# The last half pair's softmax sums are inverted on chip instead of through DRAM

## The chip, the cores and the metric

The kernel runs on one core of a Trainium2 chip. The metric is the device time of one execution in microseconds. A core has five engines with queues of their own: PE (TensorE, matmul), DVE (VectorE), ACT (ScalarE), POOL (GpSimd) and SP (SyncE, which here only issues DMAs). Each works through its queue in order, and semaphores tell one engine when another, or a DMA, is done.

## The reference

Attention with a bucket mask over 4 batches, 8 heads, 768 positions and 64 features, and behind it a gated MLP (gMLP) per batch of 768 x 512:

```python
mask = q_bucket[:, :, :, None] == k_bucket[:, :, None, :]
scores = scale * np.matmul(q, k.transpose(0, 1, 3, 2))
scores = np.where(mask, scores, -1000000000.0)
scores = scores - np.max(scores, axis=-1, keepdims=True)
attn = np.exp(scores)
attn = attn / (np.sum(attn, axis=-1, keepdims=True) + 1e-09)
x = np.matmul(attn, v)                # then heads are put side by side: (4, 768, 512)

h = x @ w_in                          # 512 -> 1024
h = 0.5 * h * (1.0 + np.tanh(c * (h + 0.044715 * h ** 3)))
u, v = (h[..., :d_ff // 2], h[..., d_ff // 2:])
v_n = (v - mu) / np.sqrt(var + 1e-06) * g_ln
v_s = np.einsum('ts,bsd->btd', w_sg, v_n) + b_sg[None, :, None]
out = x + (u * v_s) @ w_out
```

The division by the row sums is what the change touches, for 1/32 of the rows.

## The kernel before

**Attention.** Heads are worked in 16 pairs (two heads fill 128 partitions), each pair in two halves of 384 queries. For each half, `weigh` computes scores transposed (keys in partitions, queries in columns), takes the exponential on ACT into `p`, multiplies with v on PE (`av`), and adds the `p` tiles up on POOL and DVE into one `sum` tile for each head. `finish` then needs, for each query, the sum over all keys: a matmul of `sum` with a matrix of ones. Its steps (lines of the profile):

- `total` (L598): for each head the sums of 384 queries, as two times 192 columns, each copied to 32 partitions; ACT copies them to `sm` (L601), and `av` to `un` (L603).
- A trip through DRAM, to spread 768 values over all partitions: `s<-sm` (L606), `sq<-s` (L607, 128 partitions x 6 columns), 1e-9 is added (L608) and the reciprocal taken (L609) on DVE, `r<-sq` (L611), and two broadcasts `rs<-r` (L613, one for each head).
- `e` (L617, L618) on ACT, for queries that match no key; `xt = un * rs` (L619) on DVE; `xt + e` (L620) on POOL; and `xs<-xt` (L621), which stores the half's result, transposed, in DRAM.

All DMAs of this trip are issued on SP, between the loads of q, k, v and of `x`.

**MLP.** For each of the 4 batches, `load_x` loads four x tiles (L694, 128 features x 768 positions) and splits each into a high part `xh` (ACT, L699) and a low part `xl` (POOL, L697). `hidden` multiplies with w_in in three matmuls for each x tile: six tiles `ps_h` of 512 columns for the gate's input (L765), then eight of 384 columns for u (L794), with four PSUM buffers. A tile is freed once `gelu2` is done: the square `h` on ACT (L749), a product on DVE (L750), the tanh on ACT (L752), a product on DVE into `y` or `u` (L754). From y follow the normalisation (DVE L772 to L774, POOL L775, DVE L777) and its high and low parts `zh` (ACT L779) and `zl` (DVE L781). In batch 0, `gate_weights` loads w_sg into `gs` (L716, issued on ACT) and transposes it on PE (L724; ACT L730, DVE L733), b_sg goes through `gs` to `b_bc` (L707, L708), and `out_weights` splits w_out (loads `ow` L338; DVE L356 to L365; POOL L358). `gate` is L812 to L823, `project` L838 to L848, with loads `rx` (L834).

**What sets the order.** All steps are given to a planner (`Plan`), with engine, an assumed cost, a priority and the buffers read and written. It lays out each engine's queue once, from the assumed costs; on the chip the queues are fixed. Attention's SBUF pool `late` (sum, un, rs, e, xt and the p tiles) is closed when the last half pair is finished, and the MLP's pool `b3` (gs, wgh, woh, u, ow and others) opens in its place: what writes there waits for what was read there.

Of the kernel before, what the change touches and what calls it, by code (L numbers as in the profile page):

```python
# [9 lines left out]
F32 = mybir.dt.float32  # L10
# [5 lines left out]
ALU = mybir.AluOpType  # L16
# [16 lines left out]
class Plan:  # L33
# [38 lines left out]
    def add(self, engine, cost, prio, fn, r=(), w=(), dma=0, port=None, form=None, lat=0.0):  # L72

        port = engine == "POOL" if port is None else port
        g = {"e": engine, "c": cost, "p": prio, "fn": fn, "dma": dma, "n": len(self.groups), "slots": [], "port": port, "form": form, "lat": lat}
        deps, after = set(), set()
        for kind, xs in (("r", r), ("w", w)):
            for x in xs:
                b, key = x if isinstance(x, tuple) else (x, None)
                if b.slots is not None and engine != "MEM":  # L80
                    g["slots"].append(b)
                if b.first is None:
                    b.first = g["n"]
                    last, gone = b.prev
                    if b.need is not None:
                        deps.update(n for n, _, _ in b.need.uses)
                    if gone is not None:
                        gone.gone = True
                        deps.update(n for n, _, _ in gone.uses)
                    if last is not None and last.first != g["n"]:  # L90
                        after.add(last.first)
                elif b.first != g["n"]:
                    after.add(b.first)
                assert b.gone is False
                for n, k2, kind2 in b.uses:
                    if n != g["n"] and (kind == "w" or kind2 == "w") and (key is None or k2 is None or key == k2):
                        deps.add(n)
                b.uses.append((g["n"], key, kind))
        g["deps"], g["after"] = deps, after - deps
        self.groups.append(g)  # L100

# [121 lines left out]
def kernel(  # L223
# [16 lines left out]
    nc = tc.nc  # L240

    B, H, S, D = q.shape
    P = 128
    NT = S // P
    HT = NT // 2
    SH = S // 2
# [16 lines left out]
    QH2, W6 = SH // 2, SH // 64  # L263

    const = ctx.enter_context(tc.tile_pool(name="const", bufs=1))
    dram = ctx.enter_context(tc.tile_pool(name="dram", bufs=1, space=DRAM))
# [5 lines left out]
    nc.vector.tensor_copy(identr, ident)  # L272
    epsr = const.tile([P, 1], F32, name="epsr")
    nc.vector.memset(epsr, -0.5)
    ones = const.tile([P, 32], F32, name="ones")
    nc.vector.memset(ones, 1.0)
    less = const.tile([P, 1], F32, name="less")
    nc.vector.memset(less, -1.0)
# [89 lines left out]
    PE, DVE, ACT, POOL, SP = "PE", "DVE", "ACT", "POOL", "SP"  # L368
    xs = [[dram.tile([P, S], F32, name=f"xs_{b}_{hp}") for hp in range(NP)] for b in range(B)]

    plan = Plan()
# [45 lines left out]
    if True:  # L417
# [5 lines left out]
        def ps_tile():  # L423
            ps_s.list.append(plan.slot(ps_slots, lambda i: ps_s.pool.tile([P, 512], F32, tag=f"g{i}",
                                                                          name=f"g{i}_{len(ps_s.list)}", bufs=1)))
            return ps_s.list[-1]

        def dma(prio, us, fn, r=(), w=(), e=SP, lat=0.0):
            eng = nc.sync if e == SP else nc.scalar
            plan.add(e, 0.6 if e == ACT else 0.57, prio, lambda: fn(eng), r, w, dma=us, lat=lat)  # L430
# [14 lines left out]
        def row(j):  # L445
            return slice(j * D, (j + 1) * D)
# [100 lines left out]
        def weigh(st, hf, k0, prio):  # L547
# [28 lines left out]
            for i, kt in enumerate(two):  # L576
                if kt == 0:
                    continue
                e = ADDS[kt - 1]
                for j in range(2):  # L580
                    def add(j=j, i=i, e=e, first=p[0][j] if kt == 1 else sums[j]):
                        (nc.gpsimd if e == POOL else nc.vector).tensor_add(sums[j](), first()[:, :SH], p[i][j]()[:, :SH])  # L582

                    plan.add(e, 1.01 if e == POOL else 0.55, prio + 0.6, add, [p[i][j]] + ([p[0][j]] if kt == 1 else []),
                             [sums[j]], port=True)

        def finish(st, hf, prio):

            av, sums, tp = st.av, st.sum, ps_tile()
            sm, e = late.ring([P, QH2], F32, "sm", 3), late.ring([P, SH], F32, "e", 3)  # L590
            sq, rs, xt = late.ring([P, W6], F32, "sq", 3), late.ring([P, SH], F32, "rs", 3), late.ring([P, SH], F32, "xt", 2)
            V = nc.vector

            def total():
                for j in range(2):
                    for a in range(2):
                        r = 64 * j + 32 * a
                        nc.tensor.matmul(tp()[r:r + 32, :QH2], ones, sums[j]()[:, a * QH2:(a + 1) * QH2], start=True, stop=True)  # L598

            plan.add(PE, 0.6, prio, total, sums, [tp])  # L600
            plan.add(ACT, 0.32, prio, lambda: nc.scalar.copy(sm(), tp()[:, :QH2]), [tp], [sm])  # L601
            un = late.ring([P, SH + 1], F32, "un", 3)
            plan.add(ACT, 0.48, prio - 1, lambda: nc.scalar.copy(un(), av()[:, :SH + 1]), [av], [un])  # L603

            sd, sb = dram.tile([4, QH2], F32, name=f"s_{st.n}_{hf}"), plan.buf(f"s_{st.n}_{hf}", 1)
            dma(prio, 0.1, lambda eng: eng.dma_start(sd, sm()[0:P:32, :]), [sm], [sb], lat=3.6)  # L606
            dma(prio, 0.1, lambda eng: eng.dma_start(sq(), sd.rearrange("a (p c) -> (a p) c", c=W6)), [sb], [sq], lat=4.0)  # L607
            plan.add(DVE, 0.16, prio, lambda: V.tensor_single_scalar(sq(), sq(), 1e-9, op=ALU.add), [sq], [sq], port=True)  # L608
            plan.add(DVE, 0.18, prio, lambda: V.reciprocal(sq(), sq()), [sq], [sq])  # L609
            rd, rb = dram.tile([2, SH], F32, name=f"r_{st.n}_{hf}"), plan.buf(f"r_{st.n}_{hf}", 1)  # L610
            dma(prio, 0.1, lambda eng: eng.dma_start(rd.rearrange("j (p c) -> (j p) c", c=W6), sq()), [sq], [rb], lat=4.0)  # L611
            for j in range(2):
                dma(prio, 0.3, lambda eng, j=j: eng.dma_start(rs()[row(j)], rd[j].partition_broadcast(D)), [rb], [(rs, j)], lat=4.6)  # L613

            vm = late.ring([P, 1], F32, "vm", 3)
            plan.add(ACT, 0.2, prio, lambda: nc.scalar.mul(vm(), un()[:, SH:SH + 1], 1.0 / S), [un], [vm])
            plan.add(ACT, 0.62, prio, lambda: nc.scalar.activation(e(), rs(), AF.Relu, bias=less[:, 0:1], scale=2e-9), [rs], [e])  # L617
            plan.add(ACT, 0.62, prio, lambda: nc.scalar.mul(e(), e(), vm()[:, 0:1]), [e, vm], [e])  # L618
            plan.add(DVE, 0.56, prio, lambda: V.tensor_mul(xt(), un()[:, :SH], rs()), [un, rs], [xt], port=True)  # L619
            plan.add(POOL, 0.98, prio, lambda: nc.gpsimd.tensor_add(xt(), xt(), e()), [xt, e], [xt])  # L620
            dma(prio, 0.55, lambda eng: eng.dma_start(xs[st.b][st.hp][:, hf * SH:(hf + 1) * SH], xt()),  # L621
                [xt], [(xd[st.b][st.hp], hf)])

        NPAIR = B * NP
# [26 lines left out]
        for n in range(NPAIR):  # L651
            for c in range(NT):
                if c == 0:
                    prepare(n + 1)
                hf, k0, g = c // HT, 2 * (c % HT), NT * n + c
                maxima(g + AHEAD)
                weigh(sts[n], hf, k0, 2 * g)
                if c % HT == HT - 1:
                    finish(sts[n], hf, 2 * g + FINP)
# [192 lines left out]
    for b in range(B):  # L852
        p = 500 + 1000 * b
# [41 lines left out]
```

## Time and profile before

| | us |
|---|---|
| median of 3 runs | 833.68 |
| lowest and highest | 831.89, 835.25 |
| the profiled execution, its own time | 836.75 |
| its span, from the first to the last instruction | 834.9 |
| busy PE, DVE, ACT, POOL in it | 796.2, 602.9, 412.0, 391.7 |
| mean granted TensorE clock | 0.987 |

The profile is of one execution. Times in it count from the span's start. Attention's last matmul lies at 488 us, and the MLP follows to the end. A busy PE is not a PE at its peak, since matmuls overlap: the rate is read from the distance between starts. The granted clock is the share of full speed that the throttle allowed PE.

### The profile page before, as it was taken

How to read it: one execution, taken by the hardware profiler on the slowest of the kernel's cores; microseconds unless marked ns; L12 is line 12 of the kernel's file. 1: busy time of each engine (PE TensorE's matmuls, PEld its weight loads, DVE VectorE, ACT ScalarE, POOL GpSimd, SP SyncE). 2: the span in 40 equal slices, each digit the busy share in tenths (PEclk: the TensorE clock that was granted, in tenths of full speed). 3: DMA queues.
4: the chain of work that ended last, by engine and by line, in shares of the span. 5: the costliest groups of instructions: out<-in, count | busy, mean ns of one | idle time of the engine just before them, and what ended most of it. 6: DMA issues, size and time to landing. Idle time of an engine off the chain costs nothing.

```text
span 834.9 us, 15309 instructions
## 1 busy us (share of the span) xinstructions
PE 796.2 (95%) x5480; PEld 613.5 (73%) x5480; DVE 602.9 (72%) x1305; ACT 412.0 (49%) x926; POOL 391.7 (47%) x406
## 2 busy tenths in 40 slices
PE   7999999989999999999999988799899999999998
PEld 5776666656666667666666547789689989988996
DVE  7899899997999797677677539889944248516730
ACT  2565656645655656565656745533434135314511
POOL 0566766665765655675666862234204201611030
PEclk9999999999999999999999999799999999999999
DMA  6033233223324223213301233320033230131003
GB/s 164 14 80 81 70 81 103 74 77 77 85 60 121 61 60 87 67 52 85 87 28 41 88 108 115 128 67 29 26 108 101 70 101 1 38 102 51 1 1 126
DMA packets 99308, 60.94 MB, mean 73 GB/s; under 512 B 64288, under 2 KB 91040, under 8 KB 99232
## 3 DMA queue, kind: packets, MB, share of 16 engines
q1 hardware_dynamic: 97920, 56.94, 24.3%
q10 hardware_dynamic: 1312, 3.02, 1.1%
q8 instruction: 43, 0.70, 0.4%
q14 instruction: 33, 0.27, 0.1%
HBM read 47.16 MB, written 12.78 MB: 72 GB/s over the span
## 4 chain that ended last, share of the span: by engine, by line
PE 76%; DVE 16%; DMA 4%; issue 1%; SPq 1%; POOL 1%; ACT 1%; DVEq 0%; ACTq 0%; POOLq 0%
PE g L561 15%; PE av L573 14%; PE ps_vs L812 10%; PE g L517 8%; PE ps_o L838 8%; PE ps_h L794 6%; PE ps_h L765 4%; DVE mx L524 4%; PE g L497 4%; PE g L475 2%; PE g L539 1%; PE g L598 1%; PE ps_o L843 1%; DMA q<-in_q_dram 1%; DVE wx L359 1%
## 5 line engine op out<-in xcount | busy, mean ns | idle before, releaser
L582 POOL TENSOR_TENSOR sum<-sum,p 128x384 f32<-128x384 f32 x192 | 200.4, 1067 | 69.5 <-ACT p L567 40.9
L524 DVE TENSOR_REDUCE mx<-g 128x1 f32<-128x384 f32 x384 | 188.2, 548 | 52.8 <-PE g L517 52.6
L567 ACT ACTIVATE p<-g 128x384 f32<-128x384 f32 x384 | 159.4, 500 | 123.7 <-PE g L561 121.1
L573 PE MATMUL av<-p,v 128*64 128x385 f32 x768 | 146.7, 504 | 0.0
L582 POOL TENSOR_TENSOR sum<-p,p 128x384 f32<-128x384 f32 x64 | 64.4, 1027 | 62.9 <-ACT p L567 62.8
L573 PEld LDWEIGHTS av<-p,v 128*64 128x64 f32 x768 | 47.0, 136 | 54.4 <-issue 51.5
L750 DVE SCALAR_TENSOR_TENSOR h<-h,ps_h 128x384 f32<-128x384 f32 (+1 forms) x56 | 33.0, 607 | 74.0 <-ACT h L749 73.7
L517 PE MATMUL g<-fk,fq 64*128 64x384 f32 x384 | 76.3, 371 | 4.3 <-DVE mx L524 4.0
L561 PE MATMUL g<-hq,hk 64*128 64x384 f32 x384 | 77.7, 384 | 2.0 <-DVE mx L524 2.0
L561 PEld LDWEIGHTS g<-hq,hk 64*128 64x128 f32 x384 | 39.3, 188 | 41.4 <-DVE mx L524 20.9
L517 PE MATMUL g<-hk,hq 64*128 64x384 f32 x384 | 69.2, 337 | 0.0
L561 PE MATMUL g<-hq,lk 64*128 64x384 f32 x384 | 68.4, 338 | 0.0
L561 PE MATMUL g<-fq,fk 64*128 64x384 f32 x384 | 68.2, 337 | 0.0
L561 PE MATMUL g<-lq,hk 64*128 64x384 f32 x384 | 68.1, 337 | 0.0
L812 PE MATMUL ps_vs<-wgh,zh 128*128 128x384 f32 x192 | 64.6, 336 | 2.2 <-DVE gt L815 1.4
L775 POOL TENSOR_TENSOR mv<-mv,epsr 128x1 f32<-128x1 f32 x24 | 14.0, 584 | 111.4 <-DVE mv L774 103.1
L838 PE MATMUL ps_o<-woh,gs 128*128 128x512 f32 x192 | 65.5, 402 | 0.0
L812 PE MATMUL ps_vs<-wgh,zl 128*128 128x384 f32 x192 | 64.4, 335 | 0.7 <-DVE zl L781 0.7
L812 PE MATMUL ps_vs<-wgl,zh 128*128 128x384 f32 x192 | 64.2, 334 | 0.0
L517 PEld LDWEIGHTS g<-fk,fq 64*128 64x128 f32 x384 | 40.0, 184 | 32.5 <-ACT p L567 8.4
L823 POOL TENSOR_TENSOR gs<-gt,gs 128x384 fp32r<-128x384 f32 x32 | 32.8, 1028 | 61.7 <-ACT gs L820 61.7
L794 PE MATMUL ps_h<-xh,wih 128*128 128x384 f32 x128 | 45.2, 353 | 7.7 <-DVE y L754 4.0
(127 smaller groups left out, 1708.7 us busy)
## 6 DMA issues: line engine op xcount, KB each, us to landing
q<-in_q_dram SPq DMA_DIRECT2D x32, 192.0 KB
k<-in_k_dram SPq DMA_DIRECT2D x32, 192.0 KB
v<-in_v_dram SPq DMA_DIRECT2D x16, 384.0 KB
rs<-r SPq DMA_DIRECT2D x64, 96.0 KB
xs<-xt SPq DMA_DIRECT2D x32, 192.0 KB
x<-xs SPq DMA_DIRECT2D x16, 384.0 KB
rx<-xs SPq DMA_DIRECT2D x96, 64.0 KB
out_dram<-ob SPq DMA_DIRECT2D x24, 256.0 KB
```

The source lines that it names most:

```text
L497: nc.tensor.matmul(fp()[:, :SH], w[:, s, :], x()[:, cs], start=(i == 0), stop=(i == 2))
L517: nc.tensor.matmul(sc[kh][j]()[:, :SH], x[0]()[row(j), qs], x[1]()[row(j), kh * SH:(kh + 1) * SH], start=(n == 0), stop=(n == 1))
L524: plan.add(DVE, 0.56, prio, lambda j=j, kh=kh: nc.vector.tensor_reduce(mx()[:, kh, i, j:j + 1], sc[kh][j]()[:, :SH], axis=AX.X, op=ALU.max ...
L561: nc.tensor.matmul(sc[i][j]()[:, :SH], x()[row(j), ks], y()[row(j), cs], start=(n == 0), stop=(n == 3))
L567: plan.add(ACT, 0.53, prio, lambda i=i, j=j: nc.scalar.activation(p[i][j]()[:, :SH], sc[i][j]()[:, :SH], AF.Exp), [sc[i][j]], [p[i][j]])
L573: nc.tensor.matmul(av()[row(j), :SH + 1], st.v()[:, j, kt, :], p[i][j](), start=(kt == 0), stop=(kt == NT - 1))
L582: (nc.gpsimd if e == POOL else nc.vector).tensor_add(sums[j](), first()[:, :SH], p[i][j]()[:, :SH])
L750: plan.add(DVE, us + 0.07, prio, lambda: nc.vector.scalar_tensor_tensor(h2()[:, :n], h2()[:, :n], 1.0 / GA, ps()[:, :n], op0=ALU.add, op1= ...
L765: nc.tensor.matmul(ps(), x()[:, ts_], w[:, c, FH:FF], start=(c == 0 and n == 0), stop=(c == NC - 1 and n == 2))
L794: nc.tensor.matmul(ps()[:, :SH], w[:, c, fs], x()[:, cs], start=(c == 0 and n == 0), stop=(c == NC - 1 and n == 2))
L812: nc.tensor.matmul(vp(), z()[:, t, fs], w()[:, t, cs], start=(t == 0 and n == 0), stop=(t == NT - 1 and n == 2))
L838: nc.tensor.matmul(po(), a()[:, ts_], w()[:, f, :], start=(f == 0 and n == 0), stop=False)
```

## The change

For the second half of the last pair (`quick`), `total` gives the sums of all 384 queries of a head in one matmul to all 64 partitions of that head (so `ones` has 64 columns instead of 32). DVE adds 1e-9 out of PSUM into `rs` and takes the reciprocal there, in all 384 columns. The copy to `sm`, the two DVE instructions on `sq` and the five DMAs of the trip fall away for this half. The other 31 halves are done as before, the first half of the same pair too. A line in the planner keeps a step from depending on itself.

```diff
-    ones = const.tile([P, 32], F32, name="ones")
+    ones = const.tile([P, D], F32, name="ones")
...
+            quick = st.n == NPAIR - 1 and hf == 1
+            if quick:
+                def whole():
+                    for j in range(2):
+                        nc.tensor.matmul(tp()[row(j), :SH], ones, sums[j](), start=True, stop=True)
+
+                plan.add(PE, 0.75, prio, whole, sums, [tp], form="col")
+                plan.add(DVE, 0.55, prio, lambda: V.tensor_single_scalar(rs(), tp()[:, :SH], 1e-9, op=ALU.add), [tp], [rs])
+                plan.add(DVE, 2.5, prio, lambda: V.reciprocal(rs(), rs()), [rs], [rs], port=True)
+            else:
                 def total():
...
             un = late.ring([P, SH + 1], F32, "un", 3)
             plan.add(ACT, 0.48, prio - 1, lambda: nc.scalar.copy(un(), av()[:, :SH + 1]), [av], [un])
+            if not quick:
                 sd, sb = dram.tile([4, QH2], F32, name=f"s_{st.n}_{hf}"), plan.buf(f"s_{st.n}_{hf}", 1)
                 dma(prio, 0.1, lambda eng: eng.dma_start(sd, sm()[0:P:32, :]), [sm], [sb], lat=3.6)
...
                 for j in range(2):
                     dma(prio, 0.3, lambda eng, j=j: eng.dma_start(rs()[row(j)], rd[j].partition_broadcast(D)), [rb], [(rs, j)], lat=4.6)
```

The planner lays out the queues anew. Up to the last half pair's `total` they are the same on every engine; from there on they differ at some places. Lines of the changed file stand 1 to 13 further down (L762 is the old L749, L765 in its ACT rows the old L752, L778 the old L765, L807 the old L794). The numbers behind the names tell buffers apart: h_0, h_1, h_2 are the first MLP tiles in the GELU, e_7276 and e_7229 belong to the first half of the last pair, e_7240 to the second.

ACT, behind the split of batch 0's last x tile, before:

```order
L699 CAST xh_7216<-x_7189 128x768
L749 ACTIVATE h_0_7245<-ps_h_7205 128x512
L749 ACTIVATE h_1_7255<-ps_h_7218 128x512
L752 ACTIVATE h_0_7245<-h_0_7245 128x512
L752 ACTIVATE h_1_7255<-h_1_7255 128x512
L617 ACTIVATE e_7276<-rs_7231,less 128x384
L618 ACTIVATE e_7276<-e_7276,vm_7135 128x384
L749 ACTIVATE h_2_7294<-ps_h_7251 128x512
```

Here the GELU of two tiles stands ahead of the first half's e. ACT at the same place, changed:

```order
L712 CAST xh_7194<-x_7185 128x768
L630 ACTIVATE e_7229<-rs_7200,less 128x384
L631 ACTIVATE e_7229<-e_7229,vm_7133 128x384
L630 ACTIVATE e_7240<-rs_7202,less 128x384
L631 ACTIVATE e_7240<-e_7240,vm_7173 128x384
L762 ACTIVATE h_0_7247<-ps_h_7214 128x512
L765 ACTIVATE h_0_7247<-h_0_7247 128x512
L762 ACTIVATE h_1_7267<-ps_h_7236 128x512
L762 ACTIVATE h_2_7292<-ps_h_7258 128x512
L720 DMA gs_7294<-in_moe_b_sg_dram 128x768
L765 ACTIVATE h_1_7267<-h_1_7267 128x512
L729 DMA gs_7303<-in_moe_w_sg_dram 128x768
```

Both halves' e moved ahead of the GELU, and the loads into gs moved in between its steps; before, the first of them stood behind the square of h_6.

PE, in the first two tiles of batch 0's MLP (xl_7177 and xh_7071 belong to the second and third x tile), before:

```order
L765 MATMUL ps_h_7205<-wih,xl_7177 128x512
L765 MATMUL ps_h_7218<-wih,xh_6923 128x512
L765 MATMUL ps_h_7218<-wil,xh_6923 128x512
L765 MATMUL ps_h_7218<-wih,xl_7010 128x512
L765 MATMUL ps_h_7205<-wih,xh_7071 128x512
```

The two tiles take turns as x tiles come in: six matmuls of the second stand ahead of the first one's last. PE at the same place, changed:

```order
L778 MATMUL ps_h_7214<-wih,xl_7175 128x512
L778 MATMUL ps_h_7214<-wih,xh_7069 128x512
L778 MATMUL ps_h_7214<-wil,xh_7069 128x512
L778 MATMUL ps_h_7214<-wih,xl_7191 128x512
L778 MATMUL ps_h_7214<-wih,xh_7194 128x512
```

The first tile is now computed to its end before the second is begun.

PE, where batch 0's output projection (ps_o) begins behind u tiles of batch 1, before:

```order
L794 MATMUL ps_h_8331<-xh_7710,wih 128x384
L794 MATMUL ps_h_8331<-xl_7744,wih 128x384
L794 MATMUL ps_h_8331<-xh_7710,wil 128x384
L838 MATMUL ps_o_8362<-woh_7570,gs_7801 128x512
L838 MATMUL ps_o_8362<-wol_7581,gs_7801 128x512
```

The projection follows a whole tile. PE at the same place, changed:

```order
L807 MATMUL ps_h_8323<-xh_7693,wil 128x384
L807 MATMUL ps_h_8358<-xh_7583,wih 128x384
L807 MATMUL ps_h_8358<-xl_7608,wih 128x384
L807 MATMUL ps_h_8358<-xh_7583,wil 128x384
L807 MATMUL ps_h_8358<-xh_7599,wih 128x384
L807 MATMUL ps_h_8358<-xl_7629,wih 128x384
L807 MATMUL ps_h_8358<-xh_7599,wil 128x384
L851 MATMUL ps_o_8370<-woh_7558,gs_7792 128x512
```

The first six matmuls of one more u tile of batch 1 moved ahead of the projection.

More of the change, by code (lines that the diff above doesn't have):

```diff
@@ L98, in add @@
                 b.uses.append((g["n"], key, kind))
+        deps.discard(g["n"])
         g["deps"], g["after"] = deps, after - deps
@@ L592, in finish @@
             V = nc.vector
[L594 to L601, printed above, removed]
+            quick = st.n == NPAIR - 1 and hf == 1
@@ new lines, in finish, with total @@
+            if quick:
[6 more added lines that the diff above has]
+            else:
+                def total():
+                    for j in range(2):
+                        for a in range(2):
+                            r = 64 * j + 32 * a
+                            nc.tensor.matmul(tp()[r:r + 32, :QH2], ones[:, :32], sums[j]()[:, a * QH2:(a + 1) * QH2], start=True, stop=True)
+                plan.add(PE, 0.6, prio, total, sums, [tp])
+                plan.add(ACT, 0.32, prio, lambda: nc.scalar.copy(sm(), tp()[:, :QH2]), [tp], [sm])
@@ L602, in finish @@
             un = late.ring([P, SH + 1], F32, "un", 3)
             plan.add(ACT, 0.48, prio - 1, lambda: nc.scalar.copy(un(), av()[:, :SH + 1]), [av], [un])
[L605 to L613, printed above, removed]
+            if not quick:
+                sd, sb = dram.tile([4, QH2], F32, name=f"s_{st.n}_{hf}"), plan.buf(f"s_{st.n}_{hf}", 1)
+                dma(prio, 0.1, lambda eng: eng.dma_start(sd, sm()[0:P:32, :]), [sm], [sb], lat=3.6)
+                dma(prio, 0.1, lambda eng: eng.dma_start(sq(), sd.rearrange("a (p c) -> (a p) c", c=W6)), [sb], [sq], lat=4.0)
+                plan.add(DVE, 0.16, prio, lambda: V.tensor_single_scalar(sq(), sq(), 1e-9, op=ALU.add), [sq], [sq], port=True)
+                plan.add(DVE, 0.18, prio, lambda: V.reciprocal(sq(), sq()), [sq], [sq])
+                rd, rb = dram.tile([2, SH], F32, name=f"r_{st.n}_{hf}"), plan.buf(f"r_{st.n}_{hf}", 1)
+                dma(prio, 0.1, lambda eng: eng.dma_start(rd.rearrange("j (p c) -> (j p) c", c=W6), sq()), [sq], [rb], lat=4.0)
+                for j in range(2):
+                    dma(prio, 0.3, lambda eng, j=j: eng.dma_start(rs()[row(j)], rd[j].partition_broadcast(D)), [rb], [(rs, j)], lat=4.6)
```

## The prediction

> **What bounds the kernel now.** I read the page's slices first, then a table of busy time by stage, the chain that ended last, and the timeline of each engine between 486 and 545 us.
>
> The slices (busy tenths) show a PE that is full nearly everywhere:
>
> ```profile
> PE   7999999989999999999999988799899999999998
> ```
>
> A slice is 20.9 us. The dips to 8 and 7 from slice 24 on (480 to 543 us) are where attention ends, the first MLP batch begins and the change lies. By stage (columns: busy us and instructions of PE, weight loads, DVE, ACT, POOL; granted clock; DMA share; GB/s):
>
> ```profile
> 486.00:500.00 14.00, 9.93 (x44) 6.04 (x41) 3.53 (x8) 4.82 (x10) 8.12 (x6) 1.00 0.41 113
> 580.00:606.00 26.00, 21.77 (x104) 17.92 (x102) 24.65 (x69) 10.09 (x20) 5.72 (x11) 1.00 0.09 26
> 606.00:834.90 228.90, 225.29 (x1188) 205.03 (x1188) 103.03 (x194) 77.98 (x142) 47.98 (x46) 1.00 0.20 64
> ```
>
> From 606 PE is bound by itself. Until then PE has gaps: 9.93 of 14 us busy at the start, and 21.77 of 26 where DVE is busy for 24.65. The end moves by what PE loses before 606.
>
> The chain (start, length, who) runs through the removed trip, but not through it alone:
>
> ```profile
> 489.59 4.11 DMA x<-xs
> 493.72 0.84 ACT xh L699
> 494.63 1.82 POOL xl L697
> 496.50 1.92 PE ps_h L765 x7
> ...
> 512.74 0.33 SPq L621
> ...
> 520.25 0.33 ACTq L716
> ```
>
> The last x tile of batch 0 starts the GELU on ACT. 512.74 is the issue of the last half pair's result; behind it stand the loads that reuse its memory. PE's own stalls:
>
> ```profile
> 519.12 0.34 PE L794 MATMUL ps_h<-xl,wih 128*128 128x384 f32 x1
> 519.29 0.34 PE L794 MATMUL ps_h<-xh,wil 128*128 128x384 f32 x1
> 523.38 0.69 PE L794 MATMUL ps_h<-xh,wih 128*128 128x384 f32 x1 [3.75 <-DVE u L754]
> 523.40:526.80 3.40, 3.40 (x11) 3.40 (x12) 3.30 (x9) 2.02 (x5) 0.00 (x0) 0.50 0.90 316
> 526.80:529.40 2.60, 2.60 (x10) 2.60 (x9) 1.43 (x5) 0.49 (x1) 0.00 (x0) 0.50 0.21 72
> ```
>
> PE waits 3.75 us for DVE's first u tile, and then runs 6.0 us at a granted 0.50, which costs 3.0 us more.
>
> **The change part by part.** *Removed:* the copy of the sums, both small DVE instructions, and five DMAs on SP with their waits. On SP the last half pair's trip ran in line with everything else:
>
> ```profile
> 489.97 0.54 SPq L606 DMA_DIRECT2D s<-sm  x1
> 490.60 0.39 SPq L611 DMA_DIRECT2D r<-sq  x1
> 493.99 1.11 SPq L613 DMA_DIRECT2D rs<-r  x2
> 503.47 0.32 SPq L621 DMA_DIRECT2D xs<-xt  x1
> 512.74 0.33 SPq L621 DMA_DIRECT2D xs<-xt  x1
> ```
>
> The rows 490.60, 493.99 and 503.47 are the first half of the same pair (half 0), which still goes through DRAM. *Added:* two matmuls of 384 columns for four of 192 (the same columns in all), an addition from PSUM and a reciprocal over 384 columns on DVE. Neither is on a path: DVE idles 9.64 us before its first h (row below). For the reciprocal the nearest rows are
>
> ```profile
> L609 DVE RECIPROCAL sq<-sq x32: 191/191/194, 51.0 to 498.5; 128x6 f32<-128x6 f32 x32
> L774 DVE TENSOR_SCALAR mv<-mv x24: 147/153/156, 501.7 to 777.6; 128x1 f32<-128x1 f32 x24
> ```
>
> (191 - 153) / 5 = 7.6 ns a column makes 2.9 us; 191 / 6 would make 12.2 us. I take 2.9: much of so short an instruction is fixed. The addition passes as many columns as an xt product (543 ns, below). Started at 488.5, both are done by 492. At 12.2 us they would be done at 501.3, some 4 us after half 0's reciprocals.
>
> *Moved:* the half's tail, as the pieces of order above show. On ACT four e instructions, the first of which waits for half 0's reciprocals, went ahead of the square of h_0 (the first step of the GELU; on DVE both xt products went ahead of h_0 likewise), and the square of h_2 and a load went ahead of the tanh of h_1. On PE the second MLP tile no longer fills the first one's waits for x. The sum needs these rows:
>
> ```profile
> 482.75 3.58 DMA rs<-r
> 497.03 0.60 ACT L749 ACTIVATE h<-ps_h 128x512 f32<-128x512 f32 x1 [2.48 <-PE ps_h L765]
> 497.66 0.69 DVE L750 SCALAR_TENSOR_TENSOR h<-h,ps_h 128x512 f32<-128x512 f32 x1 [9.64 <-ACT h L749]
> 500.33 0.60 ACT L617 ACTIVATE e<-rs,less 128x384 f32<-128x384 f32 x1
> 501.48 0.58 ACT L749 ACTIVATE h<-ps_h 128x512 f32<-128x512 f32 x1
> L619 DVE TENSOR_TENSOR xt<-un,rs 128x384 f32<-128x384 f32 x2 | 1.1, 543 | 0.0
> 520.14 0.85 DVE L708 COPY b_bc<-gs 128x768 f32<-128x768 f32 x1 [0.33 <-DMA gs<-in_moe_b_sg_dram]
> 521.44 0.75 DVE L781 SCALAR_TENSOR_TENSOR zl<-y,mv,zh 128x512 fp32r<-128x512 f32 x1 [0.45 <-ACT zh L779]
> ```
>
> - (a) GELU starts later, +2.8. Without s on SP, half 0's r goes out 0.6 us earlier than 490.60, and rs with it: 493.4, the second 0.55 later, 3.58 to land: 497.5. Two pairs of e, 1.15 each (500.33 to 501.48), put h_0 at 499.8 instead of 497.03. Bounds: +1.2 (one pair, if rs landed when h_0 was ready) and +6.7 (the 12.2 us reciprocal).
> - (b) DVE work that leaves the GELU's stretch (497.7 to 523.7): two xt, 1.1, and one sq pair, 0.4: -1.5. It now runs while DVE idles.
> - (c) Late in that stretch DVE waited 0.33 and 0.45 because the loads behind 512.74 held up ACT. They go out from about 501 now: -0.8 (0 if they hold up ACT there).
> - (d) New waits inside the GELU. By 496.5 PE had done six matmuls of its second tile. At 1.92 / 7 = 0.27 each (496.50) they make the next tiles 1.6 us later, and the square of h_2, ahead of the tanh of h_1, waits for the third. I take +1.6; 0 if DVE is still behind then, +4.2 with 2.6 of a clock drop (below).
> - So the first u tile, on which PE waited at 523.38, comes 2.8 - 1.5 - 0.8 + 1.6 = 2.1 us later.
> - (e) PE reaches that wait later too, since it has stalled before for x and for tiles 4 and 5. Its idle time there shrinks from 3.75 to about 2.3, too short, I think, for the clock to fall in full: of the 3.0 us lost at 0.50 I take back half, -1.5; from 0 to -3.0.
> - (f) Six 384-column matmuls of batch 1 moved ahead of batch 0's output projection (third place of the order), into 580 to 606 where PE idles 26 - 21.77 = 4.2 us: six at 0.17 (519.12 to 519.29), -1.0; from 0.
>
> Sum: +2.1 - 1.5 - 1.0 = -0.4. The earlier gate weights give nothing by themselves: PE transposes them from 534.63, long after the loads of 515 to 523, and waits there for DVE.
>
> ```profile
> 534.63 0.94 PE L724 MATMUL ps_h<-ident,gs 128*128 128x128 f32 x6
> 538.86 0.67 PE L724 MATMUL ps_h<-ident,gs 128*128 128x128 f32 x3 [3.28 <-DVE u L754]
> ```
>
> The profiled execution's span of 834.9 becomes 834.5, and its time of 836.75 (1.85 more than the span) becomes 836.35. That execution is 3.1 above the median of 833.68, which becomes 833.3.
>
> [...] In the trace it stays at 1.00 in 493.4 to 497 with 1.40 of 3.6 us busy, and falls after 3.75 us of nothing:
>
> ```profile
> 493.40:497.00 3.60, 1.40 (x5) 0.76 (x5) 0.00 (x0) 0.83 (x1) 1.81 (x1) 1.00 0.61 161
> 519.60:523.40 3.80, 0.05 (x2) 0.02 (x1) 3.02 (x6) 2.10 (x4) 0.35 (x1) 0.91 1.03 337
> ```
>
> [...]
>
> **The rivals.** *Slower: the clock falls at the start.* PE now has eleven matmuls (3 us at 0.27) between 488.3 and 496.5, in pieces that wait for xl, for xh (until 494.56) and for xl again (until 496.45). The trace shows neither a fall nor safety for so little. If the clock falls by 496.5 and stays down as long as at 523.4, tiles 1 and 2 end 2.6 us later; the square of h_2 is ahead of the tanh of h_1, so (d) is +4.2, the wait before u stays as long as it was, and (e) and (f) give nothing: 2.8 - 1.5 - 0.8 + 4.2 = +4.7, 838.4. It decides if the granted clock is under 0.75 between 496.5 and 503. Against it: no stretch of 3 us is without a matmul.
>
> *Faster: both PE stalls go.* A second stall, of 3.28 us (538.86), came from two DVE instructions of 1.74 and 1.79 us, which elsewhere take 0.2 to 0.3 (the last row), while POOL ran xl:
>
> ```profile
> 534.17 3.69 POOL L697 TENSOR_TENSOR xl<-x,xh 128x768 fp32r<-128x768 f32 x2 [3.87 <-ACT xh L699]
> 534.45 1.74 DVE L361 TENSOR_SCALAR owy<-owx 128x128 int32<-128x128 int32 x1
> 536.22 1.79 DVE L362 SCALAR_TENSOR_TENSOR owy<-ow,owy 128x128 f32<-128x128 uint32 x1
> 542.75 0.29 DVE L362 SCALAR_TENSOR_TENSOR owy<-ow,owy 128x128 f32<-128x128 uint32 x1
> ```
>
> If the shifted order lets them pass at other times (3.0) and (e) is full, -0.4 - 3.0 - 1.5 = -4.9, 828.8. Against it: the same kinds of instructions stand there.
>
> *The reciprocal costs 12.2 us:* (a) is +6.7, +3.5 in all, 837.2. Of 32 small ones none took over 194 ns, so I expect no wait for POOL on top.
>
> *Nothing changes:* were half 0's trip, not half 1's, what held the memory, no load would move; its result went out at 503.47, 9.3 us ahead of 512.74, so this is out.
>
> **Chances.** Forecast 0.61 (830 to 836.5), faster rival 0.16, clock 0.18, reciprocal 0.05. The range from 828.0 to 839.0 takes in both ends. About 0.5% (4.2 us) is what a measurement of this kernel can tell from no change: faster 0.16, slower 0.22 (the clock and most of the reciprocal), same 0.62.
>
> **What would show it.** The last xs issue near 500 to 501 instead of 512.74; h_0 on ACT near 499.8; the first u on DVE near 525; PE's wait before it near 2.3 us; the clock after it between 0.5 and 1. I am wrong if the clock falls by 497, if ACT's load issues hold up the GELU by more than a microsecond or two, or if PE's order after 545 moves more than six matmuls' worth.

## The result, and the profile after

| | before | after |
|---|---|---|
| median of 19 runs each, us | 833.74 | 839.12 |
| lowest and highest | 830.98, 838.34 | 833.13, 846.07 |
| profiled execution: own time, span | 836.75, 834.9 | 840.38, 838.6 |

The ratio is 1.0062, with a 95% interval of 1.0044 to 1.0081: the change makes the kernel some 5 us slower. The ratio leaves out two executions after, of 846.07 and 845.82 us, that lie over 1.5% above the fastest. The forecast was 833.3, and the range ended at 839.0.

The row of PE in the page's slices, with 7 in place of 8 in the slice from 587 to 608 us:

```profile
PE   7999999989999999999999988799799999999998
```

By stage (columns as in the prediction: busy us and instructions of PE, weight loads, DVE, ACT, POOL; granted clock; DMA share; GB/s), from 480 us to the end, first before, then after:

```profile
480.00:834.90 354.90, 332.46 (x1722) 295.99 (x1718) 204.21 (x430) 130.97 (x250) 92.58 (x97) 0.98 0.22 69
```

```profile
480.00:838.60 358.60, 336.62 (x1730) 299.00 (x1728) 205.08 (x430) 132.51 (x252) 94.35 (x98) 0.97 0.21 68
```

PE's idle time is the same, 354.90 - 332.46 = 22.4 us and 358.60 - 336.62 = 22.0. The 3.7 us between the spans are busy time of PE, and the granted clock is lower (0.97 against 0.98). By the `un` copy below, 1.1 us of them lie ahead of the MLP. The steps named in the prediction, from the timelines of after:

```profile
487.68 0.48 ACT L615 COPY un<-av 128x385 f32<-128x385 f32 x1 [3.07 <-PE av L574]
489.83 0.56 DVE L603 TENSOR_SCALAR rs<-g 128x384 f32<-128x384 f32 x1 [0.70 <-PE g L600]
490.42 2.55 DVE L604 RECIPROCAL rs<-rs 128x384 f32<-128x384 f32 x1
498.46 0.61 ACT L630 ACTIVATE e<-rs,less 128x384 f32<-128x384 f32 x1 [3.80 <-DMA rs<-r]
500.79 0.58 ACT L762 ACTIVATE h<-ps_h 128x512 f32<-128x512 f32 x1
500.85 1.48 SPq L634 DMA_DIRECT2D xs<-xt  x2
525.25 0.45 PE L807 MATMUL ps_h<-xh,wih 128*128 128x384 f32 x1 [2.03 <-DVE u L767]
```

The sums are inverted on chip by 493.0. ACT then waits until 498.46 for half 0's reciprocals, and the square of h_0 starts at 500.79. The copy `un` stands for the end of attention. It lies at 486.58 before, so 1.1 us of the later start are attention's own and not the change's.

The loss becomes visible much later, where batch 1's u tiles meet batch 0's output projection. Stages before and after:

```profile
602.00:606.00 4.00, 3.48 (x19) 3.16 (x19) 3.79 (x12) 1.20 (x4) 0.57 (x2) 1.00 0.12 33
606.00:612.50 6.50, 6.50 (x34) 5.72 (x35) 6.22 (x17) 3.11 (x7) 0.89 (x2) 1.00 0.00 1
```

```profile
602.00:605.50 3.50, 0.50 (x3) 0.18 (x2) 3.26 (x11) 1.35 (x3) 0.92 (x2) 1.00 0.00 0
605.50:612.40 6.90, 6.02 (x19) 6.02 (x20) 6.69 (x19) 3.37 (x7) 1.26 (x2) 0.51 0.07 19
```

Before, PE is busy for 3.48 of 4 us and the clock stays at 1.00. After, it is busy for 0.50 of 3.5 us and then runs 6.9 us at 0.51. In both orders four u tiles of batch 1 stand ahead of the projection. The third and the fourth each wait for one of the last two `y` of batch 1, which free PSUM buffers. These two `y`, the first matmul of each of the two tiles and the first of the projection, before:

```profile
601.61 0.67 DVE L754 SCALAR_TENSOR_TENSOR y<-h,ps_h 128x512 f32<-128x512 f32 x1
602.34 0.44 PE L794 MATMUL ps_h<-xh,wih 128*128 128x384 f32 x1 [0.83 <-DVE y L754]
605.20 0.68 DVE L754 SCALAR_TENSOR_TENSOR y<-h,ps_h 128x512 f32<-128x512 f32 x1
605.93 0.44 PE L794 MATMUL ps_h<-xh,wih 128*128 128x384 f32 x1 [0.18 <-DVE y L754]
608.12 0.40 PE L838 MATMUL ps_o<-woh,gs 128*128 128x512 f32 x1
```

After, the two `y` and the two tiles, and then the chain that ended last at this place:

```profile
598.37 0.68 DVE L767 SCALAR_TENSOR_TENSOR y<-h,ps_h 128x512 f32<-128x512 f32 x1
599.10 0.45 PE L807 MATMUL ps_h<-xh,wih 128*128 128x384 f32 x1 [0.96 <-DVE y L767]
605.65 0.68 DVE L767 SCALAR_TENSOR_TENSOR y<-h,ps_h 128x512 f32<-128x512 f32 x1
606.38 0.69 PE L807 MATMUL ps_h<-xh,wih 128*128 128x384 f32 x1 [3.89 <-DVE y L767]
```

```profile
602.03 1.06 DVE h L763 x2
603.09 0.15 DVE owy L357
...
605.53 0.20 DVE wol L366
605.73 0.61 DVE y L767
606.38 6.12 PE ps_h L807 x18
612.50 2.77 PE ps_o L851 x12
```

Ahead of the fourth tile PE waits 3.89 us, where it waited 0.18. The `y` that ends this wait is not late: counted from `un` it starts at 117.97, and at 118.62 before. PE is early. Its third tile starts at 111.42 instead of 115.76, because the `y` for that one moved ahead, and the last `y` did not move with it. Between the two `y` DVE works without a pause, for 7.28 us instead of 3.59. In between stand now two `h` (602.03 in the chain), one of them the last tile's, which stands ahead of both `y` before; seven steps on one more tile of w_out (the first 603.09, the last 605.53 in the chain); and a normalisation. PE idles little more than before between 580 and 606, 26 - 20.86 = 5.1 us instead of 4.2, but most of it in one piece, and the clock falls there. The 18 matmuls behind it, 12 of the fourth tile and the six that were moved, start 0.32 us apart in PE's timeline instead of 0.17, which costs 18 x 0.15 = 2.7 us.

### The profile page after: what moved, and what is told of

Same layout as the page of the kernel before. It is cut to its first block, busy times and chain, and to the rows that moved or that the text cites. A ratio compares the mean times of both kernels' runs of the same rounds, so it can differ in the third digit from the quotient of the medians.

```text
span 838.6 us, 15288 instructions
## 1 busy us (share of the span) xinstructions
PE 797.9 (95%) x5476; PEld 615.0 (73%) x5476; DVE 605.7 (72%) x1305; ACT 411.9 (49%) x925; POOL 392.2 (47%) x406
## 4 chain that ended last, share of the span: by engine, by line
PE 75%; DVE 18%; DMA 3%; issue 1%; SPq 1%; ACT 1%; POOL 0%; DVEq 0%; ACTq 0%; POOLq 0%
PE g L562 14%; PE av L574 13%; PE ps_vs L825 11%; PE ps_o L851 8%; PE g L518 8%; PE ps_h L807 6%; PE ps_h L778 4%; DVE mx L525 4%; PE g L498 3%; PE g L476 3%; PE g L540 1%; PE ps_o L856 1%; PE g L610 1%; DVE h L763 1%; DMA q<-in_q_dram 1%
## 5 line engine op out<-in xcount | busy, mean ns | idle before, releaser
L836 POOL TENSOR_TENSOR gs<-gt,gs 128x384 fp32r<-128x384 f32 x32 | 32.9, 1030 | 60.9 <-ACT gs L833 60.9
L633 POOL TENSOR_TENSOR xt<-xt,e 128x384 f32<-128x384 f32 x32 | 33.1, 1035 | 44.4 <-issue 25.9
```

## The experiments

Lines in the experiments' own rows are shifted: L942 there is the L762 above, L945 is L765, L947 is L767, L958 is L778, L987 is L807; in the first run with fillers L812 is L807 and L772 is L767. Edits that reorder long lists are given in words. Ratios are to before, on the same chip, with 95% intervals. The theories were: the loss lies in the queues that the planner laid out anew (A in the expectations), or in the inversion itself, on DVE or in the memory it changes.

**The change with the old queues.** The inversion is kept; the two DVE instructions stand right behind half 0's reciprocals, and all other steps stand in before's order, given as a list.

```diff
-        order = self.order()
+        self.order()
+        order = [int(n) for n in ORDER.split()]
```

> The inversion on chip is kept as in the changed kernel, but every queue is written in the order of the kernel before; the add and the reciprocal stand on VectorE right behind half 0's own reciprocal. Theory A (the loss of 5 us sits in the re-planned queues, which let TensorE idle 3.9 us at 602.5 and run two stretches of 3.4 us at half clock behind that): this kernel has none of it, 831 to 835 us, ratio to before 0.997 to 1.002. Theory B (the inversion itself costs the time: VectorE's 0.56 + 2.55 us and a GELU that starts later): 837 to 840 us, as the changed kernel.

Measured: 832.95, 0.9991 (0.9968 to 1.0013). Repeated on another chip:

> The inversion on chip with the queues of the kernel before, once more, for a tighter interval and a second profile: the first gave a ratio of 0.9991 (0.9968 to 1.0013), while from the last un to the end its profile took 345.5 us against 348.4 of the kernel before. If the 2.9 us are the change's own gain: ratio 0.996 to 0.998. If they are one execution's luck with the clock: 0.999 to 1.001.

833.7, 1.0005 (0.9986 to 1.0023). The inversion costs nothing, and gains nothing that can be measured. The loss is in the queues.

**Which part of the queues.** The same list, cut at batch 1's first hidden tile (573 us after): the changed order up to there with before's behind it, and the reverse.

```diff
+ORDER = (changed order ahead of the cut) + (before's order behind it)   # old tail
+ORDER = (before's order ahead of the cut) + (changed order behind it)   # old start
```

> The changed kernel in its own order up to batch 1's first hidden tile (573 us in its profile), and from there on all queues in the order of the kernel before: the late start stays, the order in which VectorE takes the last tiles of batch 1 and TensorE the products around 602 is undone. Theory A2 (the loss is made in that tail): no wait of 3.9 us and no half-clock stretch at 605, 834.5 to 836.5 us. Theory A1 (the late start is the loss): 837.5 to 839.5 us.

> The counterpart of the run with the old tail: the inversion on chip, all queues in the order of the kernel before up to batch 1's first hidden tile, and from there on in the order of the changed kernel. Old start with old tail stood at 833 to 833.7 us, new start with old tail at 836.9, new start with new tail at 839.1. If start and tail add up: 833.3 + 2.2 = 835.5 us (834.5 to 836.5), with the wait of some 3.9 us ahead of the 18 matmuls there again. If the tail only costs where the start was late: 833 to 834 us.

| | old tail | new tail |
|---|---|---|
| old start | 0.9991, 1.0005 | 1.0028 (1.0007 to 1.0050) |
| new start | 1.0042 (1.0020 to 1.0065) | 1.0062 (1.0044 to 1.0081) |

Both parts cost: the start 0.0034 to 0.0044 (2.8 to 3.7 us), the tail 0.0020 to 0.0030 (1.7 to 2.5 us), and within the intervals they add up to the whole. Each alone is slower than before beyond its interval; the sizes, differences of such ratios, are rough. The wait follows the tail. Old start with new tail, then new start with old tail (stages, and PE's wait ahead of the fourth u tile):

```profile
595.00:598.80 3.80, 0.00 (x0) 0.00 (x0) 3.56 (x11) 2.04 (x4) 0.59 (x2) 1.00 0.10 33
598.80:604.00 5.20, 5.12 (x20) 5.08 (x21) 4.99 (x16) 1.81 (x6) 0.95 (x2) 0.67 0.00 1
598.88 0.69 PE L987 MATMUL ps_h<-xh,wih 128*128 128x384 f32 x1 [3.88 <-DVE y L947]
```

```profile
600.00:607.00 7.00, 5.97 (x33) 5.38 (x32) 6.55 (x19) 1.91 (x4) 0.91 (x2) 1.00 0.06 19
604.70 0.45 PE L987 MATMUL ps_h<-xh,wih 128*128 128x384 f32 x1 [0.19 <-DVE y L947]
```

With the old start the clock is 1.00 up to 598.8, the end of the wait of 3.88 us, and 0.67 in the 5.2 us behind it. In the changed kernel it falls in the last microsecond of the wait of 3.89 us (1.00 up to 605.5, then 0.51 for 6.9 us). With the old tail the wait is 0.19 us, and the clock stays at 1.00. From the gate to the end the nine profiles at full clock with the changed tail and no filler in this wait, the changed kernel's and those of the runs below included, take 288.4 to 291.3 us, and the seven with the old tail and no fillers 286.4 to 288.1.

**Matmuls in the wait.** The changed kernel, with 15 matmuls whose result nobody reads put where PE waits.

```diff
+FILL = {3513: 15}   # step: matmuls behind it
...
+    def fill(count):
...
+        for _ in range(count):
+            nc.tensor.matmul(idle[0], wih[:, 0, 0:P], wih[:, 0, 0:FH], start=True, stop=True)
```

> The changed kernel with 15 further 128x128 by 128x512 matmuls, whose result nobody reads, behind the last product that stands ahead of the 3.9 us wait at 602.5. They add 15 x 0.234 = 3.5 us of TensorE work inside the wait. Theory A (of the loss, 18 matmuls at 0.32 instead of 0.17 us apart behind the wait, about 2.8 us, come from the clock that falls in the wait): clock 1.00 from 606 to 612, ps_o starts 2.5 to 2.8 us earlier, 835.5 to 837 us against 839.1. Theory B (VectorE is simply late, the clock does not set the end): 838.5 to 840 us, or more for the added work.

Measured: 836.2, 1.0042 (1.0021 to 1.0064).

```profile
604.00:608.40 4.40, 3.72 (x19) 3.37 (x20) 4.19 (x13) 1.60 (x4) 0.95 (x2) 1.00 0.02 6
604.24 0.45 PE L812 MATMUL ps_h<-xh,wih 128*128 128x384 f32 x1 [0.49 <-DVE y L772]
607.04 0.44 PE L812 MATMUL ps_h<-xh,wih 128*128 128x384 f32 x1 [0.44 <-DVE u L772]
```

The clock stays at 1.00; from the gate to the end the profile takes 287.8 us, as with the old tail. By the medians' ratios 0.0062 - 0.0042 = 0.0020 (1.7 us) come back, about what the old tail gives. The two intervals overlap, so that size is rough; that the wait took the clock is shown (0.51 for 6.9 us without the matmuls in it, 1.00 with them). The 2.7 us lost at half clock don't return in full: PE, faster, waits for DVE again at 607.04, where the six moved matmuls begin.

**Matmuls in every wait behind 513 us,** in the changed order and in the old one:

```diff
+FILL = {2821: 5, 2921: 7, 2937: 8, 2978: 13, 2996: 7, 3513: 15}   # changed order
+FILL = {2921: 4, 2937: 15, 2978: 13}   # old order
```

> The changed kernel with such matmuls in six of its waits: 5 behind the second accumulation step of the first tile of the GELU stage, 7 and 8 in the two waits between u tiles (516.9 and 523.2), 13 and 7 in the two waits of the gate weights' transposes (534.6 and 541.6), 15 at 602.5. If the clock is the whole loss (theory A at its most), no half-clock stretch is left between 490 and 830 and the time falls to 832 to 835 us. If VectorE sets the stretch from 535 to 602 whatever TensorE's clock, only what the wait at 602.5 costs comes back: 835.5 to 837 us. Theory B: 839 us or more.

> The kernel with the queues of before and the inversion on chip, with 4, 15 and 13 matmuls that nobody reads in the waits at 513.8, 519.6 and 535.6 (there 1.2, 3.75 and 3.3 us long), behind which the clock of the kernel before falls to half for 6.8 and 3.4 us. Theory A: the clock stays at 1.00 and 2 to 4 us of the time come back, 828 to 831.5 us, below both kernels. If the stretch behind them is set by VectorE and ScalarE and not by the clock: 831 to 834 us. If the added work delays what it stands ahead of: 834 to 836 us.

Measured: 837.7, 1.0059 (1.0038 to 1.0080), and 833.12, 1.0004 (0.9979 to 1.0029). The changed order with all fillers:

```profile
512.00:545.00 33.00, 30.43 (x158) 26.47 (x156) 31.33 (x70) 19.99 (x42) 8.56 (x10) 1.00 0.13 47
```

In the changed order the clock is now full from 512 to 545 us, and the gate comes no earlier: 61.4 us behind `un`, against 60.9 without fillers. DVE is busy for 31.33 of 33 us there. The median, 837.7, lies between the theories: what the filler at 602 alone gave back does not show in it, and why is not known; all these intervals overlap. In the old order the gate does come earlier, at 56.5 against 57.8 to 60.7 in four profiles without fillers, but the clock then falls at 596.6 for 6.9 us (granted 0.51), and from the gate to the end it takes 290.4 us. So the clock was not kept, the drop moved, and the time is the same.

**What in the start costs 3 us.** The changed queues begin with four differences: four e ahead of the first square, PE no longer alternating between the first two tiles, the inverted half's e late, and the loads of gs early. First, a buffer of its own for the inverted half's `rs`, since the planner otherwise holds it until half 0's copies are issued:

```diff
+            if quick:
+                rs = late.ring([P, SH], F32, "rq", 1)
```

> The changed kernel, planned anew, with a tile of its own for the inverted sums in place of the third of the ring rs. In the plan of the changed kernel the add has to follow the issue of half 0's rs (one ring, tiles taken in order), and so the planned start of the first GELU tile on TensorE stands 5.3 us later than in the plan before (492.4 against 487.1); with a tile of its own that hold is gone. If the planner's late start is what shuffled the queues: a plan near to the old one and 831 to 835 us. If any new plan is a new draw: anything from 831 to 840; 837 to 840 would leave the old order of the queues as the lucky one.

834.76, 1.0016 (0.9995 to 1.0038). The planner now lays out a start nearer to before's: two squares and a tanh stand ahead of all four e again, and h_0 starts 9.51 us behind `un`, as with the old queues (9.39). The tail is still the new one (clock 0.51 behind the wait), and the time is that of old start with new tail:

```profile
602.00:606.00 4.00, 0.33 (x2) 0.01 (x1) 3.76 (x11) 1.95 (x4) 0.87 (x2) 0.80 0.09 30
606.00:611.40 5.40, 5.24 (x16) 5.23 (x17) 5.19 (x16) 2.00 (x6) 0.95 (x2) 0.51 0.01 2
```

So the planner's hold is what put the e ahead of the GELU, and without it the time shows no loss from the start. Then single rows of the changed order were moved:

```diff
 ACT: ... xh, [e e e e], h_0, tanh, h_1, h_2, ...
+all four e behind the tanh of h_1, both xt behind batch 0's first statistics
 PE: ... tile 0, tile 1, tile 2 ...
+PE takes tiles 0 and 1 in turns, as before
+inverted half's e behind the last xh, its xt behind the reciprocal, its result stored early; half 0's e behind two squares and a tanh
+both of the last two lines
```

> The changed kernel in its own order, but for one thing: the four e of pair 15 stand on ScalarE behind the first two squares and tanh of the GELU (as in the kernel before) and the two xt on VectorE behind the first y, so the first square no longer waits for half 0's rs from DRAM. Theory A1 (the later start of the GELU, 13.1 us behind the last un against 9.4 with the old queues, is carried through to the end): the start comes 3 to 3.5 us earlier, the first u 2 to 3 us, the time 836 to 837.5 us against 839.1. Theory A2 (the start is made up for by the stretch that VectorE sets, and the loss is made behind the ps_vs, in the wait at 602.5 alone): the start is earlier, the time stays at 838.5 to 840.

> The changed kernel in its own order, but TensorE takes the first two tiles of the GELU stage in turns, as in the kernel before, so that it has steps of the second tile to do while the first waits for x. If the half clock at 496.3 and the late second tile (its square waits 0.9 us for TensorE) make the start late: 836 to 838 us. If the start hangs on the e pairs that stand ahead of the first square on ScalarE: 838.5 to 840 us.

> The changed kernel in its own order, but the inverted half's e pair, xt and store run where their data is there (behind the last xh), and half 0's e pair and xt, which wait for rs from DRAM, stand behind the first two squares and tanh: two e in the GELU in place of four, and ScalarE not held until 498.5. If the hold by half 0's rs is the late start: the first square 3 us earlier, 835.5 to 837 us. If the second tile's matmuls then hold it (one tile after the other): 837.5 to 840 us, and with all four e behind it was 842.4.

> Both edits at once, with the tail as in the changed kernel. If both halves of the start's mechanism are named with them: 834 to 835.5 us, the level of the old start with the new tail (834.45 us). If the start's loss has another cause: 837 us or more.

In turn: 842.36, 1.0112 (1.0083 to 1.0142); 838.59, 1.0083 (1.0052 to 1.0115); 841.02, 1.0098 (1.0072 to 1.0124); 839.84, 1.0083 (1.0059 to 1.0108). None repairs the start, and the first is worse than the changed kernel: in its profile h_0 starts at 9.8 instead of 13.1 behind `un`, but the first u on DVE at 43.6 instead of 37.0. What ACT waited for with both (494 to 513 us; columns: total, times, longest):

```profile
ACT h L945 <- DMA gs<-in_moe_b_sg_dram: 3.1, 1, 3.1
ACT h L942 <- DMA rx<-xs: 2.8, 1, 2.8
ACT h L945 <- DMA rx<-xs: 0.6, 1, 0.6
ACT h L942 <- DMA gs<-in_moe_w_sg_dram: 0.6, 1, 0.6
```

Each of these four waits lies right behind the issue of a load of gs, which stands in ACT's queue amid the GELU; together they hold it for 7.1 us. The loads of rx are issued on SP; the profile names them as what ended two of the waits. Next, the seven loads of gs and the copy of b_bc were put at before's places, on top of both edits and alone in the changed order:

```diff
-ACT: h_2, load gs, tanh of h_1, load gs, ...
+ACT: h_2, tanh of h_1, ...   (loads of gs where before has them)
```

> The run with both edits of the start (tiles in turns, e pairs split; 839.84 us, with 7 us of waits of ScalarE behind gs and rx loads in its profile) with the seven loads and b_bc back at their old places as well. If the loads are what made those edits worthless: 833.5 to 835.5 us, the level of the old start with the new tail. If it stays at 838 us or above, the cause of the start's loss is not among the edits named.

> The changed kernel in its own order, but ScalarE issues the seven loads of b_sg and w_sg (gs), and VectorE copies b_bc, behind the same instructions as in the kernel before, that is, behind the GELU's tiles and not between them. If the loads in the GELU are the start's loss (ScalarE issues them, and where no DMA lane is free behind the eight rx, its next square or tanh waits: 2.0 us in the changed kernel's profile): 836 to 837.5 us, the start's 3 us mostly back, the tail's 2 us not. If they only fill gaps of ScalarE, and the transposes then wait for later loads: 839 us or more.

Measured: 836.13, 1.0050 (1.0026 to 1.0074), and 837.45, 1.0061 (1.0035 to 1.0086). With the loads moved, the same view of the first has no DMA in it:

```profile
ACT h L942 <- PE ps_h L958: 4.8, 3, 1.7
ACT h L945 <- DVE h L943: 3.2, 3, 1.6
ACT zh L972 <- DVE y L970: 0.8, 1, 0.8
```

In this profile the loads no longer hold ACT, and the gate comes 4.2 us earlier (59.4 instead of 63.6, counted from `un`). So the loads can account for what moving e added (1.0083 against 1.0050, though the intervals overlap), but alone they are not the start's 3 us: moved by themselves they give nothing. With all three edits the interval holds both 1.0028 (start repaired) and 1.0062 (not). Which row of the start costs the time stays open.

**The old queues with the gain taken.** Before's order, with the inverted half's e, xt and store early, where their data is there:

```diff
+ORDER = before's, inverted half: e behind the last xh, xt behind its reciprocal, xt + e and xs right behind
```

> The inversion on chip with the old queues, but the inverted half's own e pair, xt and store stand where their data is there: e behind the last xh of the first x loads, xt behind the reciprocal, 10 to 15 us earlier than in the old queues, where half 1 still had the place of its trip through DRAM. If the place of these six instructions is what keeps the change from bringing anything: 830.5 to 832.5 us. If nothing behind them waits for them (the GELU's first u waits for VectorE's y, the transposes for u): 832.5 to 834 us, as with the old queues.

> The inversion on chip with the old queues and the inverted half's e pair early, once more for a tighter interval: 0.9994 (0.9971 to 1.0017) at first, its profile 343.7 us from the last un to the end against 346.2 and 348.4 of the kernel before. If the gain of 2.5 us is its own: 0.996 to 0.998; if it is chance: 0.999 to 1.001.

Measured: 831.99, 0.9994 (0.9971 to 1.0017), and 832.39, 0.9985 (0.9965 to 1.0005). It is faster than the changed kernel, but not measurably faster than before, or than the old queues as they are. The two profiles of this kernel show what chance does here: with a granted clock of 0.95 from 513 to 545 us the gate came 55.6 us behind `un`, with 0.79 it came at 58.8.

**Second profiles of both kernels:**

> The kernel before, unchanged, for a second profile: from the last un to the end 348.4 us in the first. 346 to 349 us, with one to three half-clock stretches of 3.4 us between 515 and 605; a value near 346 would say that the 2.9 us that the old queues with the inversion on chip showed against it are chance.

> The changed kernel, unchanged, for a second profile. If the wait at 602.5 and the half clock behind it belong to its queues and not to one execution: TensorE again waits 3.5 to 4.2 us ahead of the 18 matmuls, their spacing is again 0.32 us in most of them, and from the last un to the end it takes 350 to 353 us.

Before took 831.15. The changed kernel's execution took 1244.96, at a mean granted clock of 0.56; it tells nothing of waits at full clock, so what was expected of it is not answered. Before's second profile, at the two places:

```profile
515.00:545.00 30.00, 22.55 (x113) 20.67 (x112) 27.53 (x62) 16.98 (x36) 9.61 (x10) 0.83 0.45 156
596.00:606.00 10.00, 10.00 (x48) 9.40 (x47) 9.55 (x27) 3.82 (x9) 1.47 (x3) 0.83 0.04 13
```

From 596 to 606 us the clock is 0.83 here, and was 1.00 in the first profile; from 515 to 545 it is 0.83 in both. So where the clock falls differed between two executions of one kernel.

## Why the prediction was wrong

Times counted from the `un` copy, in us (in after, 500.79 - 487.68 = 13.11 for h_0; the other entries likewise, from timelines of PE, DVE and ACT):

| | h_0 | first u on DVE | gate weights | gate | projection | end |
|---|---|---|---|---|---|---|
| before | 10.45 | 36.19 | 48.05 | 60.67 | 121.54 | 348.36 |
| before, second | 9.94 | 35.50 | 44.69 | 58.76 | 119.35 | 346.17 |
| old queues | 9.39 | 34.52 | 43.71 | 57.83 | 118.22 | 345.48 |
| old queues, second | 9.70 | 34.80 | 45.40 | 59.63 | 118.76 | 345.99 |
| after | 13.11 | 36.97 | 46.01 | 60.94 | 124.63 | 350.88 |

- *Removed and added at no cost*: right. The addition took 0.56 us (0.55 was taken), the reciprocal 2.55 (2.9); it was no path, as the old queues show. 2.55 us / 384 is 6.6 ns a column. The rival of 12.2 us is out. Its price was also too high: +6.7 puts both pairs of e behind the reciprocal, but half 0's pair would have been done by 498.7, so that the same rows give 501.3 + 1.15 - 497.03 = +5.4.
- *(a) +2.8*: measured 13.11 - 10.45 = +2.7. Right. The store at 500.85 (500 to 501 was expected) and the first u on DVE (about 525 expected) came as said too, though 1.1 us of both are attention's own:

```profile
524.65 1.01 DVE L767 SCALAR_TENSOR_TENSOR u<-h,ps_h 128x384 f32<-128x384 f32 x2
```

- *(b), (c), (d)*: the first u on DVE came +0.8 (36.97 - 36.19) where +2.1 was predicted, but +1.5 to +2.5 against the other three profiles with the old start. PE's wait before it was 2.03 (2.3 predicted).
- *(e) -1.5* is the first term that failed. That a wait of 2.3 us is too short for the clock to fall in full was the author's estimate. In after the wait was 2.03 us, and the drop that (e) counted on was indeed gone: the clock was full from 499.7 to 537.3. But it had moved. Between 490 and 548 us the clock was at 0.50 for 10.2 us before (522.7 to 529.5 and 539.8 to 543.2) and for 13.6 after (496.3 to 499.7 and 537.3 to 547.5). In the two profiles compared the gate came only +0.3 later, near the +0.6 that the terms up to (e) give; but that is luck of the execution. Against the other three profiles with the old start it came +1.3 to +3.1 later, and the timed runs put the start at 2.8 to 3.7 us. The prediction summed against one execution, and credited the change with that execution's drop. Its reading of the drop was also rough: the row from 519.60 has a mean clock of 0.91, so that the clock had fallen by 522.7, after some 3.1 us of nothing and not 3.75.
- *(c) ACT's loads*: "0 if they hold up ACT there" was the bound that held. Earlier loads did hold ACT (497 to 513 us):

```profile
ACT h L762 <- DMA rx<-xs: 2.0, 1, 2.0
```

- *(f) -1.0*: wrong in sign, and the largest miss. From the gate to the end after takes 350.88 - 60.94 = 289.9 us against 287.7 before: +2.3. The prediction gave the six matmuls the idle 4.2 us between 580 and 606. But they stand behind the fourth u tile in PE's queue, and PE's idle time lies ahead of that tile; behind it, from 605.93 on, PE had none before, and the projection followed at 608.12. So there was nothing for them to fill. Nor did the prediction ask what DVE's new order does to PE's waits: the 0.18 us ahead of the fourth tile became 3.89, and the clock fell to 0.51 for 6.9 us. The runs changed the tail as a whole; whether DVE's order alone makes the wait was not run. That more than six matmuls' worth would move was one of the prediction's own signs: three matmuls of the gate also moved ahead of the first u tile.
- *Second stall unchanged*: right, 3.2 us against 3.28.

```profile
PE ps_h L737 <- DVE u L767: 3.2, 1, 3.2
```

- *The rival of the clock* (838.4) came nearest, and its condition half true. The start of after, in two windows of 3.4 us:

```profile
492.90:496.30 3.40, 1.24 (x3) 0.48 (x3) 0.07 (x1) 0.83 (x1) 2.05 (x2) 1.00 0.67 200
496.30:499.70 3.40, 3.09 (x7) 2.48 (x8) 1.03 (x2) 1.21 (x3) 0.26 (x1) 0.50 0.55 174
```

The clock fell by 497, as "wrong if" said, but for 3.4 us and not for 6, so that it averages 0.75 between 496.5 and 503, just at the rival's mark; the wait before u shrank all the same. The time came out near that rival's, mostly for another reason.

So the failed steps are two. (f) was +2.3 in place of -1.0 in the profile, and a loss of 1.7 to 2.5 us in the timed runs, by a wait of 3.89 us and the clock that it took; the clock's part is shown by the filler in that wait. (e), a gain of 1.5 us from a clock drop that only moved, left a start that costs 2.8 to 3.7 us in the timed runs; what in the start costs it stays open.

## What to carry to other kernels

When a planner lays the queues out anew, find the place of a moved matmul in its own queue: it can fill idle time only if the wait stands behind it. Then compare the queue of the engine that frees the buffers: its order decided here whether PE's idle time came in pieces of 0.2 to 1.6 us or in one of 3.9. Price a clock drop against more than one execution, and ask where it goes when it leaves its place (here to 537.3 us in the changed kernel, and to 596.6 with fillers in the old order). And run the edit with the old queues first: here it showed at once that the edit itself was free and the new order cost 5 us.

## What was not expected of the hardware

The clock fell behind a stretch that was not empty. In the first of the two windows from 492.90 in after, PE was busy for 1.24 of 3.4 us, and the clock was at 0.50 in the second. Before, PE was busy for 1.40 of the 3.6 us from 493.40, and the clock stayed at 1.00 there and until 522.7. The two shares, 0.36 and 0.39, lie close together; why only one of the stretches was followed by a drop was not shown.

The drops differ in length, too. Between 490 and 620 us the two profiles have five drops to 0.50: of 3.4 us (from 496.3 after, from 539.8 before), of 6.8 us (from 522.7 before, from 605.5 after) and of 10.2 us (from 537.3 after).
